# The norm's inverse root spread over the partitions: a matrix product, or two on-chip transfers in GpSimd's queue

## The chip, the cores and the metric

One core of one Trainium2 chip runs the whole program. The metric is the device time of one execution in microseconds; lower is better. The engines are called PE (matrix products), ACT (ScalarE), DVE (VectorE), POOL (GpSimd) and SP (SyncE, which here only issues transfers).

## What is computed

```python
# gated linear attention, B=4, H=8, S=768, D=48
scale = minimum(mag, 0.999) / (mag + 1e-06)          # mag = |a_re + i a_im|
for t in range(S):
    S_re, S_im = a * (S_re, S_im) + k_t v_t          # complex decay, outer product
    y[:, :, t] = einsum('bhd,bhde->bhe', q[:, :, t], S_re)
# feed-forward on x = y as (3072 tokens, 384)
rms = sqrt(mean(x * x, axis=-1) + 1e-06)
xn  = x / rms * rms_g
g   = xn @ w_gate                                    # 384 x 1536
out = (g * sigmoid(g) * (xn @ w_val)) @ w_out        # 1536 x 384
```

The change concerns the one number `1 / rms` per token. It is a column (one value per partition, tokens on partitions) where it is computed, and it is needed as a row of 128 tokens repeated on all 128 partitions, because xn is kept with features on partitions and tokens along the free axis.

## The kernel before

The 3072 tokens are cut into 24 chunks of 128 (`N = 24`, `C = 128`). Two chunks make a group (`GROUPS`), and the feed-forward runs on a group, 256 tokens at a time.

For each chunk `attend(n)` (L1101) records the attention: scores from `kq` (products in a tiling of 32 columns), a mask copy into `am` (DVE), the output `yT` in bank 6 from `am` and the old state (`am,ve` and `kq,state` products, also tiled), transposes of `k` (`ident,kq`) which ACT copies to `kt`, and the state products (`kt,vn`, tiled). Then comes the norm:

- L1173: ACT squares `yT` into `sq`, of which there is one buffer (`sqs`, L848);
- L1178 to L1180: DVE makes `yg = yT * rms_g` and adds the three parts of `sq` (in chunks 0 to 3, the units `LIGHT`, this is done in another way);
- L1184: PE sums over the partitions with a product against `ones`, giving one value per token in a column of bank 7;
- L1186: DVE scales it and adds the epsilon, into `ssv`;
- L1187: POOL raises it to the power −0.5, into `rss[n % 2]`, a column of 128x1;
- L1189 and L1190: PE multiplies that column, broadcast over 128 columns, with the identity. The result, `wide` in bank 7, has the roots of the 128 tokens along each partition's row;
- L1197: DVE multiplies `yg` with `wide` into `xT`, the feed-forward's input.

`feed(g, xT)` (L1222) records the group's products: `xT,wg` and `xT,wv` (six pairs of blocks), ACT's Silu into `sg`, DVE's product into `hT`, and the output products from `hT`, `wo` and `sums`. From group 2 on the output uses fewer products with sums of blocks (`S1` to `S4`, `T1` to `T4`).

Nothing is issued as it is recorded. Each recorded operation goes into a list with its engine, an assumed duration, what it reads and writes and sometimes a due time; `Flow.schedule` (L555) then plans all engines, and `Flow.issue` (L662) writes each engine's instructions in the planned order. A queue runs its own order without skipping. Assumed durations therefore decide the order of instructions of all engines, and a new duration or latency can move many of them. For a transfer the planner assumes an issue time, a load on 16 transfer engines and a fixed landing time (`LAND`, with 1.5 more for POOL's queue, L609). `due` times are worked back from users; `dma` (L786) gives each transfer a `land` for that.

All instructions are issued in L667, so rows of the profile differ by their tiles' names, not by line.

Of the kernel before, what the change touches and what calls it, by code (L numbers as in the profile page):

```python
# [18 lines left out]
P = 128  # L19
C = 128  # L20
# [441 lines left out]
class Flow:  # L462
# [59 lines left out]
    def add(self, eng, calls, dur, reads=(), writes=(), table=None, land=None, due=None, after=(), behind=(), late=None, mode=None):  # L522
        op = dict(i=len(self.ops), eng=eng, calls=calls, dur=dur, deps=set(), table=table, land=land,
                  base=due, late=late, mode=mode, stage=self.stage, behind={o["i"] for o in behind})
        self.ops.append(op)
        op["deps"].update(o["i"] for o in after)
        for ap in reads:
            self.note(op, ap, False)
        for ap in writes:
            self.note(op, ap, True)  # L530
        return op
# [23 lines left out]
    def schedule(self):  # L555
# [15 lines left out]
        now = 0.0  # L571
        order = 0

        def release(o, end, users=users):
            for u in users[o["i"]]:
                x = self.ops[u]
                lat = self.SYNC if x["eng"] != o["eng"] or o["land"] is not None else 0.0
                ready[u] = max(ready[u], end + lat)
                left[u] -= 1
                if not left[u]:  # L580
                    waiting[x["eng"]].append(x)

        def flows(t):
            busy = [q for q in lanes.values() if q]
            whole = sum(q[0][1]["packet"] for q in busy)
            for q in busy:
                q[0][0] -= (t - now) * q[0][1]["packet"] / whole

        while True:
            best = None  # L590
            for eng, ops in waiting.items():
                if ops:
                    t = max(free[eng], min(ready[o["i"]] for o in ops))
                    if eng == "SP" and len(sent) >= self.LANES:
                        if "landed" not in sent[-self.LANES]:
                            continue
                        t = max(t, sent[-self.LANES]["landed"])
                    if best is None or t < best[0]:
                        best = (t, eng)
            busy = [q for q in lanes.values() if q]  # L600
            if busy:
                whole = sum(q[0][1]["packet"] for q in busy)
                q = min(busy, key=lambda q: q[0][0] / q[0][1]["packet"])
                t = now + max(0.0, q[0][0]) * whole / q[0][1]["packet"]
                if best is None or t <= best[0]:
                    flows(t)
                    now = max(now, t)
                    o = q.pop(0)[1]
                    o["landed"] = now + self.LAND + (1.5 if o["eng"] == "POOL" else 0.0)  # L609
                    release(o, o["landed"])  # L610
                    continue
            if best is None:
                break
            t, eng = best
            pick = None
            for o in waiting[eng]:
                if ready[o["i"]] > t + 1e-9:
                    continue
                key = o["due"]
                if o["table"] and table not in self.TABLES[o["table"]]:  # L620
                    key += self.switch
                if eng == "PE" and o["mode"] != mode:
                    key += self.turn
                if pick is None or key < pick[0]:
                    pick = (key, o)
            o = pick[1]
            waiting[eng].remove(o)
            dur = o["dur"]
            if o["table"] and table not in self.TABLES[o["table"]]:
                table = self.TABLES[o["table"]][-1]  # L630
                dur += 1.3
                self.loads = getattr(self, "loads", 0) + 1
            if eng == "PE" and o["mode"] != mode:
                mode = o["mode"]
                dur += 0.06
            if eng == "PE" and self.warm and t < self.warm["until"]:
                since = max([free["PE"]] + [x["end"] + self.SYNC for x in self.warm["after"] if not recent])
                n = int((t - since - 0.3) / 0.43)
                if n > 0:
                    self.fillers.append((order - 0.5, n))  # L640
                    recent.append((since, since + 0.43 * n))
            if eng == "PE":
                busy = sum(min(e, t) - max(b, t - 4.0) for b, e in recent if e > t - 4.0)
                if busy < 2.0:
                    dur += min(dur, 3.0)
                recent.append((t, t + dur))
                del recent[:-12]
            o["start"], o["end"], o["order"] = t, t + dur, order
            order += 1
            free[eng] = t + dur  # L650
            release(o, t + dur, self.next)
            if o["land"] is not None:
                flows(t)
                now = max(now, t)
                if eng != "POOL":
                    sent.append(o)
                lanes.setdefault(eng, []).append([o["load"] + 0.05, o])
            else:
                release(o, t + dur)
# [10 lines left out]
def fast(tc, ctx, qT, kT, v, a_re, a_im, w_gate, w_val, w_out, rms_g, out, H, bad):  # L670
# [6 lines left out]
    N = B * NCH  # L677
# [20 lines left out]
    def room(name, shape, dtype=FP32):  # L698
        t = mem.tile(shape, dtype, name=name, tag=name)
        row = 1  # L700
        for x in shape[1:]:
            row *= x
        rooms[t.tensor.name] = (name, row * mybir.dt.size(dtype))
        keep.append(t)
        return t
# [72 lines left out]
    def run(x):  # L778
        n = 1
        for step, size in reversed([tuple(y) for y in x.ap][0 if x.tensor.name in outside else 1:]):  # L780
            if step != n:
                break
            n *= size
        return n

    def dma(o, x, eng="SP", **kw):  # L786
        n = mybir.dt.size(o.dtype)
        for s in o.shape:
            n *= s
        row = mybir.dt.size(o.dtype) * min(run(o), run(x))  # L790
        load = n / row * (0.006 + 50.3e-6 * row) / 16
        op = add(eng, [(QUEUE[eng].dma_start, (), dict(out=o, in_=x))], 0.85 if eng == "POOL" else 0.62, [x], [o],
                 land=2.0 + 1.4 * load, **kw)
        op["load"] = load
        op["packet"] = max(0.07, 0.006 + 50.3e-6 * row * (2 if eng == "POOL" and row == 2048 else 1))
        return op

    def mms(list_, dur, **kw):
        calls, reads, writes = [], [], []
        for o, l, r, start, stop in list_:  # L800
            calls.append((nc.tensor.matmul, (o,), dict(lhsT=l, rhs=r, start=start, stop=stop)))
            reads += [l, r]
            writes.append(o)
        return add("PE", calls, dur, reads, writes, **kw)
# [9 lines left out]
    ident = room("ident", [P, P])  # L814
# [34 lines left out]
    ygs = [room(f"yg{i}", [P, ND, C]) for i in range(2)]  # L849
    ssv = room("ssv", [P, N])  # L850
    rss = [room(f"rs{i}", [P, 1]) for i in range(2)]
    sgs = [room(f"sg{i}", [P, 512]) for i in range(2)]
    ots = [room(f"ot{i}", [C, DM]) for i in range(2)]
    sums = room("sums", [P, 2, HD * DH])
# [16 lines left out]
    for e in range(2):  # L871
        for b in range(4):
            x = causal[b * BLK:(b + 1) * BLK, e]
# [6 lines left out]
    for t in banks[4:6]:  # L880
        fill(t, 0.0, eng="DVE")
    dma(gcol, rms_g.rearrange("(c p) -> p c", p=P))


# [16 lines left out]
    landed = {}  # L901
# [59 lines left out]
    EARLY = {0: -100.0, 1: -98.0}  # L961
    SUMMED = ()
    LIGHT = (0, 1, 2)
    turn = {}
    moved = {}
    HOLD = 1
# [134 lines left out]
    def attend(n):  # L1101
# [12 lines left out]
        for a in range(2):  # L1114
            ps = banks[4 + a]
# [10 lines left out]
            o = am[:, a * HH:(a + 1) * HH]  # L1126
# [3 lines left out]
        ps = banks[6]  # L1130
# [3 lines left out]
        for i in range(4 * ND):  # L1134
            j, c = divmod(i, 4)
            m, r = divmod(i, 3)
            o = yT[c * BLK:(c + 1) * BLK, j]
# [10 lines left out]
        if not last:  # L1148
            kt = kts[0]
            for a in range(2):  # L1150
                ps = banks[7 - 3 * a]
# [5 lines left out]
            ps = banks[5][0:D2, 0:DM]  # L1157
# [14 lines left out]
        sq, yg = sqs[0], ygs[n % 2]  # L1172
        act(sq, yT, AF.Square)  # L1173
        if unit_of[n] in LIGHT:
            for j in range(ND):
                act(yg[:, j], yT[:, j], AF.Copy, scale=gcol[:, j:j + 1])
        else:
# [3 lines left out]
        ps = banks[7]  # L1181
        col = ps[:, C:C + 1]
        parts = range(ND if unit_of[n] in LIGHT else 1)
        mms([(col, sq[:, j], ones, j == 0, j == parts[-1]) for j in parts], 0.25 * len(parts))  # L1184
# [1 line left out]
        ts(sv, col, 1.0 / DM, EPS_RMS, ALU.mult, ALU.add)  # L1186
        add("POOL", [(nc.gpsimd.tensor_tensor, (), dict(out=rss[n % 2], in0=sv, in1=mhalf,  # L1187
                                                        op=ALU.pow))], 0.9, [sv, mhalf], [rss[n % 2]])
        wide = ps[:, 0:C]  # L1189
        mms([(wide, rss[n % 2].to_broadcast([P, P]), ident, True, True)], 0.25)  # L1190
        g = group_of[n]
        ns = GROUPS[g]
        x, lo = xplace[g]
# [127 lines left out]
    o = 0  # L1321
# [8 lines left out]
    ps = banks[7]  # L1330
# [62 lines left out]
```

## Time and profile before

| | us |
|---|---|
| median of 3 runs | 729.72 |
| lowest and highest run | 727.16 and 731.01 |
| profiled execution | 729.62 |
| its span, first to last instruction | 727.9 |

The profile comes from one execution. Its span is 1.7 us shorter than that execution's time, the rest lying around the program. Busy times are sums over an engine's instructions; PE's matmuls are pipelined, so the length of one matmul row is more than what it adds to the stream. In a row of groups, `out<-in` gives the tiles' names without numbers, `x` the count of records (a float32 product makes two records on PE), and after the bar come busy time and mean time of one. In the timeline a row is a stretch of equal instructions with its start, its length and, in brackets, the idle time ahead of it and what ended that.

The early part of the run, to about 90 us, loads and converts weights and computes the gates. From then on attention of later chunks is interleaved with the feed-forward of earlier ones.

### The profile page before, as it was taken

How to read it: one execution, taken by the hardware profiler on the slowest of the kernel's cores; microseconds unless marked ns; L12 is line 12 of the kernel's file. 1: busy time of each engine (PE TensorE's matmuls, PEld its weight loads, DVE VectorE, ACT ScalarE, POOL GpSimd, SP SyncE). 2: the span in 40 equal slices, each digit the busy share in tenths (PEclk: the TensorE clock that was granted, in tenths of full speed). 3: DMA queues.
4: the chain of work that ended last, by engine and by line, in shares of the span. 5: the costliest groups of instructions: out<-in, count | busy, mean ns of one | idle time of the engine just before them, and what ended most of it. 6: DMA issues, size and time to landing. Idle time of an engine off the chain costs nothing.

```text
span 727.9 us, 16198 instructions
## 1 busy us (share of the span) xinstructions
PE 685.7 (94%) x6906; PEld 603.7 (83%) x6906; DVE 471.6 (65%) x740; ACT 334.1 (46%) x452; POOL 42.0 (6%) x80
## 2 busy tenths in 40 slices
PE   0579999999999999999999999999999999999996
PEld 0558867877899889889899889889889889889885
DVE  6979988789897887787847737756745234134121
ACT  7649756755656765732923823822821110110010
POOL 6123100001000000000000000000000000000000
PEclk9979999999999999999999999999999999999999
DMA  8797655634545435543722303314303102200000
GB/s 285 226 304 208 193 168 170 184 106 130 170 127 147 153 93 131 171 153 99 189 82 62 97 20 91 97 34 106 81 17 73 55 12 68 65 13 2 23 1 26
DMA packets 104575, 80.64 MB, mean 111 GB/s; under 512 B 42800, under 2 KB 95280, under 8 KB 104496
## 3 DMA queue, kind: packets, MB, share of 16 engines
q1 hardware_dynamic: 100432, 64.99, 32.8%
q0 software_dynamic: 3264, 14.16, 5.5%
q8 instruction: 56, 0.92, 0.5%
q10 hardware_dynamic: 800, 0.39, 0.2%
q14 instruction: 23, 0.19, 0.1%
HBM read 55.84 MB, written 4.72 MB: 83 GB/s over the span
## 4 chain that ended last, share of the span: by engine, by line
PE 87%; DVE 5%; DMA 3%; ACT 2%; SPq 1%; issue 1%; POOL 0%; DVEq 0%; ACTq 0%
PE bank L667 87%; DMA kq<-rot 2%; SPq L667 1%; DVE turns L667 1%; DVE rot L667 1%; DVE wg L667 1%; ACT t L667 1%; DMA in<-in_a_re_dram 1%; ACT turns L667 0%; DVE t L667 0%; DVE wo L667 0%; DVE wv L667 0%; ACT L667 0%; DVE ot L667 0%; DVE in L667 0%
## 5 line engine op out<-in xcount | busy, mean ns | idle before, releaser
L667 PE MATMUL bank<-xT,wg 128*128 128x256 f32 x864 | 199.8, 381 | 1.6 <-DVE xT L667 1.5
L667 PE MATMUL bank<-xT,wv 128*128 128x256 f32 x864 | 199.1, 380 | 0.0
L667 PEld LDWEIGHTS bank<-xT,wg 128*128 128x128 f32 x864 | 163.7, 191 | 24.5 <-DVE xT L667 2.2
L667 PEld LDWEIGHTS bank<-xT,wv 128*128 128x128 f32 x864 | 163.5, 190 | 22.5
L667 PE MATMUL bank<-wo,hT 128*128 128x192 f32 (+1 forms) x576 | 125.8, 362 | 0.4 <-DVE hT L667 0.4
L667 DVE TENSOR_TENSOR hT<-bank,sg 128x512 f32<-128x512 f32 x72 | 49.6, 689 | 114.4 <-PE bank L667 102.0
L667 PEld LDWEIGHTS bank<-wo,hT 128*128 128x128 f32 x576 | 95.6, 191 | 13.7 <-issue 2.5
L667 ACT ACTIVATE sg<-bank 128x512 f32<-128x512 f32 x72 | 42.9, 596 | 132.0 <-PE bank L667 131.4
L667 ACT ACT_TABLE_LOAD x69 | 88.5, 1283 | 11.5 <-DVE rot L667 7.9
L667 ACT ACTIVATE sq<-bank 128x384 f32<-128x384 f32 x24 | 11.8, 490 | 101.2 <-PE bank L667 101.2
L667 DVE TENSOR_TENSOR rot<-kin,turns 128x768 f32<-128x768 f32 x48 | 44.8, 953 | 14.9 <-DMA kq<-rot 14.5
L667 POOL TENSOR_TENSOR rs<-ssv,mhalf 128x1 f32<-128x1 f32 x24 | 17.2, 717 | 575.4 <-DVE ssv L667 575.4
L667 ACT ACTIVATE kt<-bank 128x384 f32<-128x384 f32 x40 | 18.4, 488 | 60.0 <-PE bank L667 59.8
L667 PE MATMUL bank<-sums,hT 128*128 128x192 f32 x240 | 45.0, 329 | 0.0
L667 ACT ACTIVATE turns<-in 128x768 f32<-128x768 f32 (+1 forms) x39 | 29.9, 789 | 21.0 <-DVE rot L667 12.5
L667 PEld LDWEIGHTS bank<-sums,hT 128*128 128x128 f32 x240 | 39.5, 190 | 0.0
L667 PEld LDWEIGHTS bank<-kq 96*32 96x32 f32 x1536 | 30.3, 111 | 10.4 <-issue 7.7
L667 DVE COPY_PREDICATED am<-causal,bank 128x512 f32<-128x512 int32 x48 | 33.3, 722 | 8.4 <-PE bank L667 8.4
L667 DVE TENSOR_TENSOR hT<-hT 128x768 f32<-128x768 f32 x40 | 38.2, 954 | 0.9
L667 PE MATMUL bank<-am,ve 128*32 128x128 f32 x768 | 38.1, 281 | 0.0
L667 PE MATMUL bank<-kq 96*32 96x96 f32 (+3 forms) x1536 | 34.7, 238 | 3.6 <-DMA kq<-rot 3.6
L667 PE MATMUL bank<-rot 128*128 128x128 f32 x64 | 11.7, 342 | 24.8 <-DVE rot L667 24.8
(112 smaller groups left out, 750.5 us busy)
## 6 DMA issues: line engine op xcount, KB each, us to landing
kq<-rot SPq DMA_DIRECT2D x144, 128.0 KB, 2.4
kin<-in_q_dram SPq DMA_DIRECT2D x24, 192.0 KB, 2.8
kin<-in_k_dram SPq DMA_DIRECT2D x24, 192.0 KB, 3.6
wo<-in_w_gate_dram SPq DMA_DIRECT2D x6, 768.0 KB, 4.6
out_dram<-ot SPq DMA_DIRECT2D x24, 192.0 KB, 2.3
wo<-in_w_val_dram SPq DMA_DIRECT2D x6, 768.0 KB, 5.7
wo<-in_w_out_dram SPq DMA_DIRECT2D x6, 768.0 KB, 5.4
in<-in_a_re_dram SPq DMA_DIRECT2D x11, 384.0 KB, 4.6
```

What stands on the lines that cost most here:

```text
L667: fn(*args, **kw)
```

## The change

For 18 of the 24 chunks, 4 to 21 (`SENT`), the product at L1190 is dropped. In its place stand two transfers in POOL's queue. The first writes the 128 values of `rss[n % 2]`, one per partition, into one line of 128 values on partition 0, within `sq` (its second part, which has been summed by then). The second reads that line and writes it to all 128 partitions of a new buffer `row`. The DVE multiply reads `row` in place of bank 7. Chunks 0 to 3, 22 and 23 keep the product; its assumed duration is raised from 0.25 to 0.28. The planner is told that each of these transfers lands 2.0 us later than its other rules say (`slow`), both in the planned landing and in the due times.

```diff
-                    o["landed"] = now + self.LAND + (1.5 if o["eng"] == "POOL" else 0.0)
+                    o["landed"] = now + o["slow"] + self.LAND + (1.5 if o["eng"] == "POOL" else 0.0)
...
-    def dma(o, x, eng="SP", **kw):
+    def dma(o, x, eng="SP", slow=0.0, **kw):
...
-                 land=2.0 + 1.4 * load, **kw)
+                 land=2.0 + 1.4 * load + slow, **kw)
+        op["slow"] = slow
...
+    row = room("row", [P, C])
...
+    SENT = range(4, N - 2)
+    SLOW = 2.0
...
-        wide = ps[:, 0:C]
-        mms([(wide, rss[n % 2].to_broadcast([P, P]), ident, True, True)], 0.25)
+        if n in SENT:
+            line = sq[0:1, 1]
+            dma(line, rss[n % 2], "POOL", slow=SLOW)
+            wide = row
+            dma(wide, line.unsqueeze(1).to_broadcast([1, P, C]), "POOL", slow=SLOW)
+        else:
+            wide = ps[:, 0:C]
+            mms([(wide, rss[n % 2].to_broadcast([P, P]), ident, True, True)], 0.28)
```

## The prediction

> **What bounds the kernel now.** I read the page first: engine shares, the clock row of the slices, and the chain that ended last.
>
> ```profile
> PE 685.7 (94%) x6906; PEld 603.7 (83%) x6906; DVE 471.6 (65%) x740; ACT 334.1 (46%) x452; POOL 42.0 (6%) x80
> ...
> PEclk9979999999999999999999999999999999999999
> ...
> PE 87%; DVE 5%; DMA 3%; ACT 2%; SPq 1%; issue 1%; POOL 0%; DVEq 0%; ACTq 0%
> ```
>
> PE is busy 94% of the span at full clock, and 87% of the last chain is PE's. So a microsecond taken off PE's stream counts, and a microsecond elsewhere counts only where PE waits for it. Next, what PE waits for in all, with times and longest wait:
>
> ```profile
> PE bank L667 <- DVE rot L667: 24.8, 1, 24.8
> PE bank L667 <- DMA kq<-rot: 3.6, 2, 2.6
> PE bank L667 <- DVE am L667: 2.7, 2, 1.5
> PE bank L667 <- DVE xT L667: 1.5, 3, 0.9
> PE bank L667 <- POOL rs L667: 1.0, 1, 1.0
> ```
>
> The 24.8 are the start. By the time of each wait, chunks 4 to 21 (some 160 to 645 us, the ones that change) hold only about 1.2 us of idle PE: 0.82 before one chunk's state products at 334.7, 0.26 and 0.09 before an xT product. The roots' own wait (1.0) is at 64 us, chunk 1. A hidden wait to be won is therefore nearly absent. Then the product itself, and its place in PE's timeline (start, length of the merged row, what, count of records):
>
> ```profile
> L667 PE MATMUL bank<-ident,rs x48: 272/275/509, 46.0 to 674.1; 128*128 128x128 f32 x48
> ```
>
> ```profile
> 218.21 1.14 PE L667 MATMUL bank<-sums,hT 128*128 128x192 f32 x6
> 219.18 1.14 PE L667 MATMUL bank<-hT 128*128 128x192 f32 x6
> 220.16 0.38 PE L667 MATMUL bank<-ident,rs 128*128 128x128 f32 x2
> 220.38 1.14 PE L667 MATMUL bank<-sums,hT 128*128 128x192 f32 x6
> 221.45 0.42 PE L667 MATMUL bank<-am,ve 128*32 128x128 f32 x8
> ...
> 223.02 0.40 PE L667 MATMUL bank<-kq,state 96*32 96x128 f32 x8
> 223.35 1.24 PE L667 MATMUL bank<-hT 128*128 128x192 f32 x6
> 224.43 0.49 PE L667 MATMUL bank<-ident,kq 96*128 96x96 f32 x4
> ```
>
> The lengths overlap, since matmuls are pipelined; what the stream pays is the step from start to start. A root product steps 220.16 to 220.38: **0.22 us**, not its 0.38 nor two times 0.275. The rows also price an excursion into the 32-wide tiling: a group of six steps 0.97 or 0.98 among its like, but 1.07 before the tiled am,ve (+0.09); the last tiled row steps 0.33 where the others of that block step 0.22 (+0.11); the first group after it steps 1.08 (+0.10). About 0.30 us each time.
>
> **What the Trainium skill says.** TensorEngine Tiling (Array Packing), Key Properties: changing the tiling mode drains the TensorE. The trace agrees, with the 0.30 us above. DMA: Bandwidth & Descriptors, Anatomy of one DMA — SWDGE (gpsimd) path: a GpSimd transfer has a fixed cost of about 2.0 us whatever its size. The nearest rows here are large loads from that queue, 1536 KB in 8.8 us and 768 KB in 5.0; drawn on to zero bytes that leaves 5.0 − 3.8 = 1.2 us. No transfer of a few bytes from that queue is in the trace. SBUF — State Buffer, A bandwidth-pool intuition that's wrong (but worth ruling out): a transfer of GpSimd's queue waits until VectorE gives back a shared port, since GpSimd must write its descriptors; one of 0.62 us became 3.1 us. Half seen here: the same power of 128 elements takes 0.55 us late in the run and longer where VectorE is busiest.
>
> ```profile
> 165.48 1.20 POOL L667 TENSOR_TENSOR rs<-ssv,mhalf 128x1 f32<-128x1 f32 x1 [48.65 <-DVE ssv L667]
> 173.08 2.11 POOL L667 TENSOR_TENSOR rs<-ssv,mhalf 128x1 f32<-128x1 f32 x1 [6.40 <-DVE ssv L667]
> 217.96 0.59 POOL L667 TENSOR_TENSOR rs<-ssv,mhalf 128x1 f32<-128x1 f32 x1 [42.77 <-DVE ssv L667]
> ```
>
> **The change, part by part.** The order in which the changed program's instructions stand on each engine can be read from the built program; I use that order, with durations of the trace only.
>
> *Removed:* 18 of 24 root products. 18 × 0.22 = **−4.0 us** on PE. Bank 7 is no longer written by them; no wait after 160 us names it, so nothing is taken for that.
>
> *Added on POOL:* 36 transfers, 18 of 512 B as 4-byte elements and 18 of 64 KB as 512-byte rows. POOL is busy 6%; a transfer occupies it 0.72 to 0.91 us (the load rows), so 36 × 0.8 = 29 us spread over 480 us, hidden. All the weight loads of POOL's queue stand before these transfers. The second transfer waits in POOL's queue for the first to land; behind it stands only the next chunk's power, 14 us of PE work or more later. The 16 DMA engines get 4608 more packets beside 104575; the slices show those engines at most 7 tenths busy after 160 us: nothing.
>
> *Longer chain, and whether it is covered.* Root to xT was power, product, multiply; now power, transfer, transfer, multiply. Because the planner is told of the slow transfers (L609, `slow`), it starts each chunk's attention earlier. Summing PE's step times between an odd chunk's column product (ones,sq) and its pair's first xT product: 3.2 to 4.4 us of PE work before, **14.3 to 16.1 us** after. For chunk 21, for instance, there are 14 half-products of 0.98 and two groups of transposes of 0.33, 14.4. Against it: about 0.55 from that product to the power (614.98 to 615.53 in the trace), 0.55 power, 0.55 multiply (its row: 547 ns), 0.3 for signals: 1.95. So 12.3 us remain, **6.2 us per transfer**, before PE waits. My price per transfer from issue to landing: from below 1.8 us (the 1 KB decay transfers of SP's queue), from above 2.5 + 2.5 = 5 us (the skill's lock delay, 3.1 − 0.6, on top). I take 2.5. Both ends fit in 6.2, so 0 us.
>
> *Added waits.* ScalarE's Square of the next chunk overwrites the line in sq that the second transfer reads; behind it on ScalarE stand the Silu evictions that free PE's banks. The built order leaves 14.4 to 19 us of PE work between a chunk's column product and the next chunk's attention output of the same pair, and 0.55 + 0.55 + 2 × 2.5 = 6.1 are needed: covered too, up to about 6.5 us per transfer. The multiply (DVE, L1197) now reads SBUF twice instead of a bank and SBUF; other such rows of 128x384 take 0.55 as well: 0.
>
> *Moved.* The planner reorders PE. The number of tiling changes rises from 119 to 129. Fitting all 350 step times after 130 us to counts and edges gives, for leaving am,ve, kq and the state products (kt,vn), 0.20, 0.23 and 0.09 us, next group included; for entering 0.11, 0.08 and 0.11. The exits go 16 to 23, 34 to 38, 10 to 4, the entries 22 to 23, 24 to 22, 13 to 19: 1.40 + 0.92 − 0.54 + 0.11 − 0.16 + 0.66 = **+2.4 us**. This is the term that eats most of the gain. From below it is 10 × 0.10 = +1.0, if only the visible step after each change counted; from above 5 × 0.32 + 1.5, some +3.1.
>
> *Waits that come and go.* The order no longer has the 334.7 stall (−0.8) nor the 0.3 before xT. In chunk 3 it puts the 24 state products straight behind the last four transposes, whose copy on ScalarE (0.49 us, plus signals) they need: +0.6 to +2; I take +1.0. Net **−0.1**, from −1.5 to +2.
>
> *Sum against the profiled execution:* 729.62 (span 727.9 and 1.7 around it) − 4.0 + 2.4 − 0.1 = 727.9. The median of the runs is 729.72, practically the same. Forecast **728.0 us**, −0.2%. A measurement of this kernel tells apart about 0.5%, 3.65 us; this is inside it.
>
> **The rivals.**
> 1. *The tiling changes cost little* (only +1.0) and waits shrink by all of 1.5: 729.6 − 4.0 + 1.0 − 1.5 = 725.1, faster by 0.6%. For it: the 0.22 is very regular. Against: the step times after tiled blocks are just as regular.
> 2. *The transfers are slow* and the second becomes PE's wait: decided at 6.2 us each. At 7.0 us each the nine pairs wait 14 − 12.4 = 1.6 us each: 9 × 1.6 = 14.4, so 728.0 + 14.4 = 742.4, slower by 1.7%. For it: the transfers are serial, of 4-byte pieces, in a software queue that VectorE can lock out, and POOL's power was seen to grow by 1.5 us. Against: all POOL transfers of 768 KB land in 5 to 6 us with their data.
> 3. *Nothing in all*: reordering costs 3.1 and chunk 3's stall 2.0, against 4.0 + 1.1: 729.6. Within 0.5%.
> 4. *It doesn't do what it says*: the built order shows 6 root products left and 36 transfers; excluded.
>
> **Numbers.** My forecast's case, a gain between 0.5 and 3.6 us: 0.56. Rival 1: 0.15. Rival 3: 0.14. Rival 2: 0.15. Faster by over 0.5%: 0.15 (rival 1). Within: 0.70. Slower: 0.15. The range runs from rival 1 (725.0) up to 732.5, which takes in rival 3 and the beginning of rival 2 (a wait of 0.5 us per pair); longer waits are left out.
>
> **What would show it.** In the changed profile: 12 root product records instead of 48; POOL with 36 more transfers and its busy time up by some 30 us; the row transfers landing within 2 to 4 us of issue; the multiply starting well before PE needs it, and no wait of PE on xT in chunks 4 to 21; PE's busy time down by only about 1.6 us, with more rows of tiled products between the full ones; a stall of about 1 us before chunk 3's state products. Waits of PE for xT at each odd chunk would mean rival 2; a busy time of PE down by 3 us or more, rival 1.

## The result, and the profile after

| | before | after |
|---|---|---|
| median of 20 runs, us | 729.43 | 727.57 |
| lowest and highest | 726.22 and 732.41 | 725.48 and 730.49 |
| profiled execution, us | 729.62 | 727.01 |
| its span, us | 727.9 | 725.3 |

The ratio is **0.998, interval 0.9965 to 0.9995**: a gain of 0.2%, within the 0.5% that the forecast of 728.0 us allowed for. The page of the changed kernel, engine shares first, then the clock and the chain that ended last:

```profile
PE 682.6 (94%) x6870; PEld 596.2 (82%) x6870; DVE 470.0 (65%) x740; ACT 332.3 (46%) x450; POOL 70.4 (10%) x116
...
PEclk9978999999999999999999999999999999999998
...
PE 83%; DVE 5%; DMA 4%; ACT 3%; SPq 2%; issue 1%; POOL 0%; DVEq 0%; ACTq 0%
```

PE is still the bound. It has 36 records fewer and 3.1 us less busy time; POOL has 36 instructions and 28.4 us more, and stays idle nine tenths of the time. What PE waited for (us in total, times, longest):

```profile
PE bank L667 <- DVE rot L667: 24.8, 1, 24.8
PE bank L667 <- DVE am L667: 4.0, 3, 1.6
PE bank L667 <- DMA kq<-rot: 2.9, 3, 1.5
PE bank L667 <- DVE xT L667: 1.3, 2, 0.9
...
PE bank L667 <- ACT kt L667: 0.7, 1, 0.7
```

The waits for `xT` did not grow, although a longer chain now leads to it. One of the two, 0.4 us at 232.2, falls among the changed chunks, but not because of the row, which had landed 6.7 us before its multiply. ScalarE waits for neither transfer. The two transfers and the roots, by their tiles (count: durations, then first and last start), with the last line of each answer, the time from issue to landing; first `rs`, then `row`:

```profile
L667 POOL TENSOR_TENSOR rs<-ssv,mhalf x24: 550/1262/1271, 44.4 to 669.9; 128x1 f32<-128x1 f32 x24
L667 POOL DMA_DIRECT2D sq<-rs x18: 582/587/862, 143.9 to 604.8; - x18
...
L667 PE MATMUL bank<-ident,rs x12: 273/275/582, 45.0 to 671.7; 128*128 128x128 f32 x12
...
DMA to landing us min/median/max: 1.9/2.0/5.9
```

```profile
L667 POOL DMA_DIRECT2D row<-sq x18: 534/534/551, 150.1 to 607.0; - x18
...
DMA to landing us min/median/max: 3.8/3.9/4.4
```

The root products are 12 records instead of 48. The gather takes 2.0 us, the spread over the partitions 3.9, though it moves only 64 KB. The longest gather, 5.9, is chunk 4's. Its stretch and that of a quick one, chunk 6's; behind the busy times of PE, PE's weight loads, DVE, ACT and POOL stand the granted clock, the busy share of the 16 DMA engines and GB/s:

```profile
143.89:149.78 5.89, 5.89 (x32) 5.17 (x31) 3.19 (x4) 5.78 (x8) 0.59 (x1) 1.00 0.95 273
197.49:199.42 1.93, 1.93 (x10) 1.70 (x9) 1.93 (x4) 0.60 (x1) 0.58 (x1) 1.00 0.01 0
```

The traces of all kernels that gather in GpSimd's queue say the same: 78 gathers beside DMA engines that the other queues keep less than 10% busy took 1.96 us in the median, 79 beside engines at least 30% busy took 2.0 to 6.2, median 2.7. The timelines of chunk 21 show how soon the row is needed after it lands. POOL's:

```profile
603.21 1.26 POOL L667 TENSOR_TENSOR rs<-ssv,mhalf 128x1 f32<-128x1 f32 x1 [16.66 <-DVE ssv L667]
604.77 0.59 POOL L667 DMA_DIRECT2D sq<-rs  x1 [0.29 <-POOL rs L667]
607.02 0.53 POOL L667 DMA_DIRECT2D row<-sq  x1 [1.66 <-DMA sq<-rs]
```

And DVE's over the same stretch:

```profile
602.98 0.15 DVE L667 TENSOR_SCALAR ssv<-bank 128x1 f32<-128x1 f32 x1
...
612.58 0.61 DVE L667 TENSOR_TENSOR mid<-mid,bank 128x192 f32<-128x192 f32 x2
613.11 0.55 DVE L667 TENSOR_TENSOR xT<-yg,row 128x384 f32<-128x384 f32 x1
615.96 0.56 DVE L667 TENSOR_TENSOR ot<-bank,mid 128x384 f32<-128x384 f32 x1 [2.30 <-PE bank L667]
```

The row lands at 607.02 + 3.9 = 610.9 and the multiply's turn in DVE's queue comes at 613.1, so 2.2 us are left there, the slack of the row at DVE. PE's first `xT` product follows at 616.7. Over the 14 chunks whose landing is in the trace, the slack is 0.9 to 6.7 us, median 4.1.

**Where the 2.6 us of span come from.** The starts of two traces differ by waits for loads, and runs of one kernel lie up to 3 us to either side of their median. So I add up PE's steps from start to start from the first product of group 1's feed to the end, where all 18 chunks lie, apart from its waits. The plain rate of a product is its step among products of its own kind, 0.216 us for one of `xT`:

| from group 1's feed on, us | before | after | difference |
|---|---|---|---|
| steps at the plain rate of their kind | 579.0 | 574.3 | −4.7 |
| what the steps took beyond that | 20.6 | 21.9 | +1.3 |
| waits | 2.5 | 2.8 | +0.3 |

The −4.7 are 18 products at 0.22, −4.0, and state products of chunk 3 that now stand ahead of this stretch, −0.7; those save nothing, since group 1's feed starts 0.7 later. With that later start and 0.2 us less behind PE's last product, the −3.1 of this stretch are the −2.6 of the span. The second row grows with the tiling changes, of which this stretch has 102 before and 110 after.

### The profile page after: what moved, and what is told of

It reads as the page before. It is cut to its first block, busy times and chain, and to the rows that moved or that the text cites. A ratio compares the mean times of both kernels' runs of the same rounds, so it can differ in the third digit from the quotient of the medians.

```text
span 725.3 us, 16217 instructions
## 1 busy us (share of the span) xinstructions
PE 682.6 (94%) x6870; PEld 596.2 (82%) x6870; DVE 470.0 (65%) x740; ACT 332.3 (46%) x450; POOL 70.4 (10%) x116
## 4 chain that ended last, share of the span: by engine, by line
PE 83%; DVE 5%; DMA 4%; ACT 3%; SPq 2%; issue 1%; POOL 0%; DVEq 0%; ACTq 0%
PE bank L667 83%; DMA ve<-in_v_dram 2%; SPq L667 2%; ACT turns L667 1%; DVE rot L667 1%; DVE turns L667 1%; DMA wo<-in_w_gate_dram 1%; ACT t L667 1%; ACT L667 1%; DMA kq<-rot 1%; DVE hT L667 1%; DMA in<-in_a_re_dram 1%; DVE in L667 0%; DVE t L667 0%; DVE wo L667 0%
## 5 line engine op out<-in xcount | busy, mean ns | idle before, releaser
L667 PE MATMUL bank<-xT,wv 128*128 128x256 f32 x864 | 201.2, 382 | 0.4 <-DVE xT L667 0.4
L667 PEld LDWEIGHTS bank<-xT,wv 128*128 128x128 f32 x864 | 161.3, 190 | 23.5 <-issue 1.6
L667 PE MATMUL bank<-wo,hT 128*128 128x192 f32 (+1 forms) x576 | 117.7, 356 | 0.6 <-DVE hT L667 0.6
L667 POOL TENSOR_TENSOR rs<-ssv,mhalf 128x1 f32<-128x1 f32 x24 | 25.3, 1054 | 498.6 <-DVE ssv L667 468.2
L667 ACT ACTIVATE turns<-in 128x768 f32<-128x768 f32 (+1 forms) x39 | 30.1, 791 | 26.5 <-DVE rot L667 14.2
L667 PE MATMUL bank<-kq 96*32 96x128 f32 (+3 forms) x1536 | 35.2, 235 | 3.0 <-DMA kq<-rot 2.9
L667 ACT ACTIVATE t<-t 128x768 f32<-128x768 f32 (+1 forms) x39 | 30.9, 792 | 8.7 <-DVE t L667 8.2
```

The lines of the kernel that those rows point to most:

```text
L667: fn(*args, **kw)
```

## The experiments

My theory: a product is worth some 0.2 us because PE is the bound; the transfers are hidden by the lead that the planner gives them; the new order's tiling changes give part of the gain back. The rivals: the product's time was partly a wait that returns elsewhere; the gain is one of order, not of the product; the transfers are near their limit. In all diffs the lines are put against the changed kernel, or against the kernel before where the text says so.

### The products put back, in the new order: `e1_products_back`

```diff
+            extra.append((nc.tensor.matmul, (ps[:, 384:384 + C],),
+                          dict(lhsT=rss[n % 2].to_broadcast([P, P]), rhs=ident, start=True, stop=True)))
...
-                mms(list_, dur, due=clock[0])
+                op = mms(list_, dur, due=clock[0])
+                op["calls"] = extra + op["calls"]
```

> The changed kernel's order on every engine, and its transfers; in addition the 18 root products are issued, two in front of each group's first feed products, into columns of bank 7 that nothing reads. So it has the new order and the old work of PE. My theory: each product costs 0.22 us, so 18 x 0.22 = 4.0 us over the changed kernel (727.6), 731.5, which is about 2 us slower than before: the price of the new order alone. Rival (the product ran in PE's slack and the small gain has another cause): no difference to the changed kernel, 727.6. Rival (reordering costs nothing and a product is worth only 0.1 us): 729.4, equal to before.

Measured: 731.1 us, ratio 1.0023 (1.0006 to 1.0040), span 728.9. The span is 3.6 above the changed kernel's, and so is the stretch from group 1's feed on (602.5 against 599.0): **0.20 us for each product**, close to the 0.22 expected. With the products in it, the new order is no better than the old one, so the gain is the product's. By the ratio it is even behind the old one, by 0.4 to 2.9 us. In the stretch it is behind by 0.4 (602.5 against 602.1), although 0.7 us of state products now stand ahead of it; like for like that is 1.1, where 2 were expected.

### The products left out of the old order: `e2_products_gone_old_order`

Against the kernel before:

```diff
+    row = room("row", [P, C])
+    fill(row, 1.0, late=LATE)
+    GONE = range(4, N - 2)
...
-        mms([(wide, rss[n % 2].to_broadcast([P, P]), ident, True, True)], 0.25)
+        op = mms([(wide, rss[n % 2].to_broadcast([P, P]), ident, True, True)], 0.25)
+        if n in GONE:
+            op["calls"] = []
...
+        if n in GONE:
+            op["calls"][0][2]["in1"] = row.unsqueeze(1).to_broadcast([P, ND, C])
```

> The order of the kernel before on every engine, with nothing in place of the 18 root products of chunks 4 to 21: the multiply into xT takes a constant row of ones, so the norm's scaling is left out for these chunks. This is the removal alone, with no transfer and no reordering. My theory: 4.0 us below before, 725.4 (ratio 0.9945), so 2 us below the changed kernel as well, the difference being what the reordering costs. Rival (reordering costs nothing): equal to the changed kernel, ratio 0.998. Rival (the old order also waited for the roots): more than 5 us below before.

Measured: 727.97 us, ratio 1.0001 (0.9979 to 1.0023), span 726.1. **A miss**: 725.4 was expected, and the runs show no gain. In the trace PE's steps did fall by 3.9 (599.6 to 595.7), but its waits in the same stretch rose from 2.5 to 4.6. What it waits for now:

```profile
PE bank L667 <- DVE xT L667: 3.1, 6, 1.2
```

Before, this row stood at 1.5 in 3 waits. A further 0.5 us is the wait for the state products of one chunk, 0.8 before and 1.3 now. In the old order the chain to `xT` has almost no lead over PE's need; taking 0.22 us of PE work out of it brings PE to the wait earlier. So the lead that the new order gives the transfers is not only a price: without a lead, about half of the product's time came back as waits.

### The same, with the planner told: `e8_products_gone_replanned`

As the last, with the assumed duration of the products at 0:

```diff
-        mms([(wide, rss[n % 2].to_broadcast([P, P]), ident, True, True)], 0.25)
+        op = mms([(wide, rss[n % 2].to_broadcast([P, P]), ident, True, True)], 0.0 if n in GONE else 0.25)
```

> As the kernel with the products gone in the old order (a constant row in place of the roots for chunks 4 to 21, so the norm's scaling is left out there), but the planner is told that the product takes no time, and makes its own order; no lead is added for the chain. Tiling changes 113 where before has 119. My theory (in the old order about 2 us of the 4.0 came back as PE's waits for xT and state products, because the chain from column product to xT has no lead): still waits, so 2 to 3.5 us below before, 725.4 to 726.9. Rival (the old order was only stale): the full 4.0 and the six tiling changes of 0.2 as well, 5.2 us below, 723.7. Rival (PE is limited by something else than its products): no gain.

Measured: 725.92 us, ratio 0.9952 (0.9933 to 0.9971), span 724.7, within what was expected. Its steps are the lowest of all, 595.0, with 96 tiling changes, but PE waits 4.2 us in 7 times for `xT`. So even a root row that costs nothing is worth about 3.5 us here (0.48%). The changed kernel's 0.2% is rather less than half of that by the ratios; by the spans of the two traces it is 2.6 of 3.2.

### The price of an excursion: `e4_extra_excursions` and `e4c_full_width_control`

45 products of 32 columns are put into gate products of groups 2 to 10, once in the 32-wide tiling (above), once at full width (below):

```diff
+    tiny = (nc.tensor.matmul, (banks[7][0:BLK, 480:512],),
+            dict(lhsT=ident[:, 0:BLK], rhs=ident[:, 0:BLK], start=True, stop=True))
...
+                if 2 <= g <= 10 and w_ is wg and b:
+                    op["calls"] = op["calls"][:3] + [tiny] + op["calls"][3:]
```

```diff
+    tiny = (nc.tensor.matmul, (banks[7][:, 480:512],),
+            dict(lhsT=ident, rhs=ident[:, 0:BLK], start=True, stop=True))
```

> The changed kernel with 45 tiny extra products: in groups 2 to 10 each of five gate products gets, in its middle, one product of 128 rows, 32 columns of weights and 32 of data (ident by ident, into columns of bank 7 that nothing reads). Each is an excursion into the 32-wide tiling and back. My theory: two tiling changes cost 0.2 to 0.3 us, and the product itself some 0.05, so 45 x 0.25 to 0.35 = 11 to 16 us over the changed kernel. Rival (a change costs the 0.06 us that the planner assumes): 45 x (0.12 + 0.05) = 8 us at most. Rival (tiling changes are free and only products cost): 45 x 0.05 = 2 us.

> The control to the 45 excursions: at the same 45 places a product of 32 columns in the full 128-wide tiling, so the tiling does not change. The excursions cost 15.9 us in span, 0.353 each, product included. My theory (most of it is the two tiling changes): a full-width product of so few columns steps about 0.14 us as the column product does, 45 x 0.14 = 6.3 us over the changed kernel, 734 us. The difference, some 0.2 us per excursion and more if the tiled product is cheaper than the full one, is the tiling's. Rival (any odd product in the stream costs 0.35): 743 us, as with the excursions.

Measured: tiled 742.91 us, ratio 1.0199 (1.0172 to 1.0227); full width 736.84, ratio 1.0126 (1.0079 to 1.0173). The spans, 741.2 and 732.6, differ by their starts too: group 1's feed begins at 119.1 and 117.5. From that feed on the two are 16.2 and 9.3 us above the changed kernel, **0.36 and 0.21 us each**. All 45 places agree: from the product ahead of the tiny one, four starts follow each other at 309, 52, 126 and 320 ns where a plain product steps 216; in the control at 216, 28, 112 and 299. So the control was too cheap in my expectation (0.14). The tiling's own part of an excursion, two changes, is 0.15 us if the tiled product costs what the full one does. It may cost less: with two steps of 17 ns, as wider products in the `kq` rows have, the part is 0.36 − 0.03 = 0.33. So one change costs 0.08 to 0.16 us. That changing the tiling costs time is confirmed, and its size is below what my fit had given.

### The planner told of less: `e3_slow_zero` and `e5_planned_as_quick`

```diff
-    SLOW = 2.0
+    SLOW = 0
```

In the second, `SLOW = -2.0`.

> One number of the changed kernel: SLOW is 0 in place of 2.0, so the planner expects each transfer to land 2 us earlier. The transfers took 2.0 and 3.9 us in the profile, the whole from the column product to the end of the multiply about 9.1 us; the new order leaves at least 10.4 us of PE work for it, so no wait of PE for xT. Tiling changes 131, their cost from the fitted prices 19.6 us where the changed kernel has 20.4. My theory (the order's tiling changes and what little waits there are set the time): about 0.8 us below the changed kernel, 726.8. Rival (the transfers are on the edge, and the extra slack is what keeps PE from waiting): slower than the changed kernel by 5 us or more, with waits of PE for xT at the second chunk of each pair.

> The changed kernel with SLOW at -2.0 in place of 2.0: the planner takes a transfer to land 4 us earlier than in the changed kernel. Then only 6.4 to 7.4 us of PE work stand between the second column product of a pair and the pair's first xT product, where the real chain (signal, root, transfers of 2.0 and 3.9 us, multiply) takes about 9.1 us in the changed kernel's profile. My theory: PE waits 1.7 to 2.7 us for xT in each of nine pairs, 15 to 24 us over the changed kernel, 743 to 751. Rival (a transfer is hidden anyway, the lead given by the order doesn't matter): within 2 us of the changed kernel.

At 0: 725.81 us, ratio 0.9966 (0.9947 to 0.9984), span 724.9. The expected 726.8 would have been no different; the interval overlaps that of the changed kernel, so the two aren't told apart. The slack of the row at DVE is down to a median of 0.76 us, and four multiplies waited for it, 5.2 us in all. PE waited hardly more for `xT` (1.6 us in 3 times).

At −2.0: 773.18 us, ratio 1.0579 (1.0528 to 1.0629), span 774.2. The direction is right and the size is not (743 to 751 expected). What PE waited for:

```profile
PE bank L667 <- DVE xT L667: 23.1, 9, 4.9
PE bank L667 <- DVE sq L667: 5.1, 4, 1.8
PE bank L667 <- DVE ot L667: 5.0, 2, 2.6
```

And the row of DVE's own list of waits that names the transfers:

```profile
DVE xT L667 <- DMA row<-sq: 64.6, 18, 6.0
```

All 18 multiplies wait, 3.6 us on average. DVE runs its queue in order, so what stands behind each is late as well, and PE then waits for `ot` and the `sq` of a later chunk too, which need nothing of the row. That is the first half of the miss: PE's waits from group 1's feed on rose by 32 us. The second half is in PE's timeline after such a wait:

```profile
184.11 4.14 PE L667 MATMUL bank<-xT,wg 128*128 128x256 f32 x12 [3.16 <-DVE xT L667]
188.05 3.20 PE L667 MATMUL bank<-xT,wv 128*128 128x256 f32 x12
191.08 2.75 PE L667 MATMUL bank<-xT,wg 128*128 128x256 f32 x12
```

Twelve records step 3.94 after the wait, 3.03 in the next row, and 2.59 once settled. The table by stretches, in columns as above:

```profile
178.00:184.00 6.00, 2.95 (x72) 1.95 (x70) 3.70 (x9) 3.94 (x6) 0.54 (x1) 1.00 0.58 101
184.00:188.00 4.00, 3.89 (x12) 3.25 (x13) 3.96 (x6) 0.00 (x0) 0.00 (x0) 0.69 0.82 225
188.00:191.00 3.00, 3.00 (x13) 2.54 (x12) 1.20 (x1) 1.88 (x2) 0.00 (x0) 0.84 0.81 204
191.00:196.00 5.00, 5.00 (x25) 4.41 (x24) 2.73 (x4) 3.55 (x5) 0.00 (x0) 1.00 0.25 54
```

These are means. Taken finer, the granted clock is 1.00 until 185.5, **0.50 from there to 188.9**, and 1.00 again, and `xT` products that lie within such a stretch step 0.427 us in place of 0.216. From group 1's feed on there are six, four of 3.4 us and two of 6.8, 27.3 us in all; each began during a wait of 2.6 to 4.9 us or within 1.5 us of its end. Another wait of 2.6 us had none behind it. Steps beyond the plain rate rose from 21.9 to 36.5 us, +15; 27.3 us at half the clock explain at most 13.7 of that.

The Trainium skill has this in TensorE: Matmul & The Clock Gate, What's actually happening: after an idle window of about 3.4 us PE runs at half rate until it has been busy for such a window. The half rate and the 3.4 us agree with the trace. The wait doesn't: 2.6 us was enough here, while in `e6_best` below a wait of 3.1 us is followed by a clock of 1.00. What decides between these, the runs leave open.

### The transfers made slower, in the same order: `e9_one_hop_more` and `e10_three_hops_more`

One or three more transfers of 512 B stand between the two, unknown to the planner; the order of all engines is that of the changed kernel.

```diff
+    HOPS = 1
...
-            dma(wide, line.unsqueeze(1).to_broadcast([1, P, C]), "POOL", slow=SLOW)
+            op = dma(wide, line.unsqueeze(1).to_broadcast([1, P, C]), "POOL", slow=SLOW)
+            other = sq[0:1, 2]
+            hops = [(other, line), (line, other), (other, line)][:HOPS]
+            op["calls"] = [(nc.gpsimd.dma_start, (), dict(out=o, in_=x)) for o, x in hops] + [
+                (nc.gpsimd.dma_start, (), dict(out=wide, in_=other.unsqueeze(1).to_broadcast([1, P, C])))]
```

> The changed kernel's order, with one more transfer in each serial chain: the line of 512 B is copied to the next line on partition 0 before it is spread. About 2.3 us more, issue and signal included, so 11.4 us in all where the order has 14.3 to 16.1 us of PE work. My theory: still hidden, within 1 us of the changed kernel, 727.6. Rival (the chain is already at the edge): 9 x 2 = 18 us more.

> The same with three more transfers in each chain: 9.1 + 3 x 2.3 = 16.0 us. My theory: past the edge in every pair; waits of 0.4 to 1.5 us for xT in nine pairs, 10 us in all, and some more where PE then runs slowly for a few microseconds, as it did after the waits in the kernel planned as quick: 737 to 745. If transfers are hidden however long they take: 727.6.

Measured: one hop 729.02 us, ratio 1.0011 (0.9994 to 1.0029), span 726.3. That is outside the 1 us expected, though its interval still touches the changed kernel's. Four multiplies already wait for the row, 4.4 us in all, but PE does not feel it: its waits for `xT` are the 1.3 us in 2 times of the changed kernel. From group 1's feed on it waits 2.2 us more, for `hT` at 226.8 and `sq` at 330.3, each over 60 us behind the last multiply that waited. So the runs do not show that one hop costs time through the row.

Three hops **766.73 us, ratio 1.0511** (1.0472 to 1.0551), span 765.4: **a miss**, 737 to 745 were expected. The median hop took 2.0 us:

```profile
sq<-sq POOLq DMA_DIRECT2D x54, 0.5 KB, 2.0
```

By medians the five transfers take 3 × 2.0 + 2.0 + 3.9 = 11.9 us; summed chunk by chunk they take 10.4 to 17.9, median 13.0. One of the chunks on DVE:

```profile
304.04 0.74 DVE L667 COPY_PREDICATED am<-causal,bank 128x512 f32<-128x512 int32 x1
307.90 0.56 DVE L667 TENSOR_TENSOR xT<-yg,row 128x384 f32<-128x384 f32 x1 [3.12 <-DMA row<-sq]
308.38 0.55 DVE L667 TENSOR_TENSOR state<-state,decay 96x384 f32<-96x384 f32 x1
308.85 0.72 DVE L667 COPY_PREDICATED am<-causal,bank 128x512 f32<-128x512 int32 x1
```

The second `am` copy needs nothing of the row, and stands behind the multiply that does. PE's list of waits shows all of it:

```profile
PE bank L667 <- DVE xT L667: 11.5, 7, 3.1
PE bank L667 <- DVE sq L667: 7.7, 4, 3.8
PE bank L667 <- DVE am L667: 6.1, 4, 3.1
PE bank L667 <- DVE ot L667: 5.5, 2, 3.5
```

The waits for `xT` are the smaller part (of those for `am`, 4.0 stood there before). Against the changed kernel, from group 1's feed on, waits rose by 26.5 us and the steps by 12.8. Half-rate stretches add up to 20.5 us, so they explain at most 10.2 of the 12.8; one of them follows a wait of only 1.9 us.

### Another queue: `e7_sp_queue`

```diff
-            dma(line, rss[n % 2], "POOL", slow=SLOW)
+            dma(line, rss[n % 2], "SP", slow=SLOW)
...
-            dma(wide, line.unsqueeze(1).to_broadcast([1, P, C]), "POOL", slow=SLOW)
+            dma(wide, line.unsqueeze(1).to_broadcast([1, P, C]), "SP", slow=SLOW)
```

> The changed kernel with both transfers in SP's queue in place of GpSimd's. My theory: they land in about 1.8 us (as the decay transfers of that queue) and 3 to 4 us, covered by the same lead; the wait for the first holds up the loads behind it in that queue by 2 us, which are early. So within 2 us of the changed kernel, 727.6. Rival (the loads of k, q and v behind it come late): PE waits for those loads, 5 us or more slower. If mixing with transfers is what makes the power on GpSimd take 1.26 us in the changed kernel, it goes back to 0.55.

Measured: 727.24 us, ratio 0.9972 (0.9954 to 0.9989), span 723.9: not told apart from the changed kernel. The tiles' answers give nearly the same landing times as in GpSimd's queue, first `sq`, then `row`:

```profile
DMA to landing us min/median/max: 1.9/2.0/4.4
```

```profile
DMA to landing us min/median/max: 3.9/4.1/4.4
```

What differs is the issue: GpSimd's queue starts the spread 0.3 us after the gather has landed, SP's up to 3.5 us after it. Two multiplies wait there for the row. The power still takes 1.19 to 1.21 us in 16 of 24 cases, so the transfers in its queue are not what makes it long.

### A version meant to be better: `e6_best`

```diff
-    turn = 0.0
+    turn = 0.3
...
-    SENT = range(4, N - 2)
-    SLOW = 2.0
+    SENT = range(4, N)
+    SLOW = 0
```

`turn` makes the planner add this much for a change of tiling.

> SLOW at 0, the transfers in chunks 4 to 23 (the last pair too), and the planner charges a tiling change 0.3 when it chooses. Tiling changes 131. My theory: against the kernel with SLOW at 0 alone (724.9 us of span), two more products go (0.44 us) and the last pair's wait of 0.9 us for xT goes, since its chain gets a lead of its own: a span of about 723.6, 725.3 in all, ratio 0.9945. Rival: the last pair has too little other work to hide the chain of 9 us, and PE waits there 3 us or more: not faster than the kernel with SLOW at 0.

Measured: 727.91 us, ratio 0.9987 (0.9968 to 1.0006), span 728.7. **A miss**: the steps are 0.2 below the changed kernel's, with 114 tiling changes in spite of the charge, and the waits 2.5 above, most of them in one wait of 3.1 us for `hT`, in this row:

```profile
PE bank L667 <- DVE hT L667: 3.8, 3, 3.1
```

It was meant to reach 725.3. The last pair's wait for `xT` did go, as foreseen. No version tried with the full computation is shown to be faster than the changed kernel; `e3_slow_zero` has the lowest ratio.

## Why the prediction was right, and where it wasn't

- **The product removed**, −4.0: right. 0.20 (`e1_products_back`) to 0.22 each.
- **The tiling changes**, +2.4: this term was mis-sized. It measured **+1.3**, between its lower end and its middle. The step that failed is the fit of step times to kinds of entries and exits, 0.20 and 0.23 us for the two commonest exits; the excursion experiment gives 0.08 to 0.16 for one change, and two of the ten counted lie ahead of group 1's feed. PE's busy time fell by 3.1 and not 1.6 mostly for that reason, which I had named as a mark of rival 1.
- **Waits**, −0.1: +0.3 from group 1's feed on. The stall that the old order had in the middle is gone, small ones came in its place, and the one foreseen for chunk 3 came just ahead of that feed, 0.67 us in place of 1.0:

```profile
119.09 0.54 PE L667 MATMUL bank<-vn,kt 128*32 128x48 f32 x24 [0.67 <-ACT kt L667]
```

  The prediction's span change of −1.7 and the measured −2.6 differ by 0.9: −1.1 and +0.4 are these two misses, and −0.2 lies behind PE's last product. The runs alone, which put the gain at 0.4 to 2.6 us, could not show misses of this size; the traces do. (In the prediction single waits are dated from the trace's zero, 10.5 us earlier than the timeline: its 334.7 is 324.2 there, its 64 is 53.5.)
- **Rival 1** (cheap changes, fewer waits) is right in its first half only: the waits didn't shrink, so 725.1 wasn't reached.
- **The transfers hidden**: right for this kernel, on half-wrong reasons. The Trainium skill, DMA: Bandwidth & Descriptors, Anatomy of one DMA — SWDGE (gpsimd) path, gives about 2.0 us as the fixed cost. The 4-byte gather agrees with 2.0; the row to 128 partitions doesn't, with 3.9, and I had priced both at 2.5. Together that is 5.9 against 5.0.
- **The 16 DMA engines, priced at nothing**: the count was too high (GpSimd's queue has 1152 packets more, not 4608), and the load of the other queues does matter. Beside it a gather took up to 5.9 us, over my upper bound of 5; the slack took it up.
- **"6.2 us per transfer, before PE waits"**: this step is wrong, though the result didn't rest on it. I worked the deadline out from PE's first `xT` product. The multiply's place in DVE's queue comes earlier: 613.1 against 616.7 in chunk 21. With one hop the transfers' sum is above my 2 × 6.2 = 12.4 in chunk 4 alone, and yet four multiplies wait. With three hops the formula of rival 2, nine waits of PE of the sum less 12.4, gives some 5 us; the run waits at DVE in all 18 chunks, four of them with sums of 12.4 or less, and loses 39 us. That price was too low because work behind the multiply is late too, and because PE runs slower after some of its waits. The slack at DVE, 0.9 to 6.7 in the changed kernel, I had not worked out; that it was enough everywhere is partly luck.
- **The price's upper bound, VectorE's lock** (the Trainium skill, SBUF — State Buffer, A bandwidth-pool intuition that's wrong (but worth ruling out)): no spread of the changed kernel took more than 4.4 us from issue to landing. In chunk 21 DVE is idle from 605.1 to 611.4 and the spread of 607.0 takes the usual 3.9, so that figure isn't the lock. The power, which I had at 0.55, is where the lock shows: in chunk 21 it takes 1.26, and this DVE row (two instructions of 0.96) begins just ahead of it:

```profile
603.10 1.95 DVE L667 TENSOR_TENSOR hT<-hT 128x768 f32<-128x768 f32 x2
```

  In `e3_slow_zero` the same power starts at 605.06 with DVE idle and takes 0.56:

```profile
605.06 0.56 POOL L667 TENSOR_TENSOR rs<-ssv,mhalf 128x1 f32<-128x1 f32 x1 [12.06 <-DVE ssv L667]
```

  In all 13 traces I sorted the 312 powers by what runs on DVE as they start. The 157 with a DVE operation of over 0.9 us in progress, its operands in SBUF and reductions apart, took 1.13 us or more, and nine in ten of them ended 0.40 to 0.43 us after that operation; the 155 without took 0.92 at most, nearly all 0.55 to 0.60. The page says that GpSimd and a two-port DVE operation can't use SBUF at once, one blocks; the power agrees. It cost nothing here, since the 0.7 us lie in the slack.

  Transfers were held far less. Beside idle DMA engines, gathers take 1.95 us in the median with long DVE operations in progress and 1.97 without. The exceptions stand beside one kind, the tensor-scalar `t<-t` on 128x768: the issue then takes 0.86 us in place of 0.59, ends 0.12 after that operation, and the gather lands after 2.2 to 3.5. One of these is chunk 15's gather with 3.3, and that chunk has the least slack, 0.9.

## What to carry to other kernels

On a kernel bound by one engine, work moved off that engine is worth its step in the stream, but only as far as the chain it belonged to has lead; without lead part of the time comes back as waits (`e2_products_gone_old_order`: 3.9 us of steps removed, 1.8 us of span won in the trace, none shown by the runs). For a slower chain the deadline isn't when the bound engine needs the result: a delay starts when the instruction that takes the result over comes up in its own engine's queue, since whatever stands behind it is late too. Small delays can be absorbed on the way (one hop: 4.4 us at DVE, no longer wait of PE for `xT`), larger ones grow (three hops: 39 us). And when a planner or scheduler reorders the stream, count what the new order costs by itself, by a run that has the new order and the old work. Compare single traces over a stretch that begins after the loads: by its span, the control of the excursions seemed to cost 0.16 us a product, by the stretch 0.21.

## What was unexpected of the hardware

- A 64 KB transfer that spreads one line of partition 0 over 128 partitions took 3.9 us in GpSimd's queue and 4.1 in SP's, twice the 2.0 us of the 512 B transfers; between issue and landing the queue made little difference.
- A 512 B gather took 2.0 us in the median beside idle DMA engines, and up to 6.2 beside busy ones.
- Waits of 1.9 to 4.9 us were followed by stretches of 3.4 or 6.8 us at half the granted clock, with matmul steps of 0.427 us in place of 0.216, but not every time: one of 3.1 us was not. Two kernels whose PE was made to wait some ten times lost up to 10 and 14 us to these stretches, beside the waits.
- POOL's power of 128 values takes 0.56 us with VectorE idle and 1.2 to 1.3 with a long tensor operation of VectorE in progress; the planner's order decides which.
- A change of tiling costs 0.08 to 0.16 us, and a lone full-width product of 32 columns put between others 0.21 us, as much as a root product of 128 columns.
